# First batch's keys and queries loaded as 1152-byte pieces into w2's room, unpacked by copies and put in order at the multiplication; weight tiles taken in at other places

## The chip, the cores and the metric

The kernel runs on one core of a Trainium2 chip. The metric is the time of one execution on the device, in microseconds (us). Three executions of the kernel before gave 483.38, 480.39 and 482.63 us, median 482.63. A fourth was profiled: 480.19 us, of which 478.5 lie between its first and last instruction (the span). All times inside the kernel below are from that execution, counted from the start of the span.

## The reference

An attention-like recurrence over 4 batches, 8 heads, 768 steps and head dimension 48, followed by a mixer on 384 = 8 x 48 channels. Inputs are fp32 for q, k, v and f_logit as the profile's shapes show; the mixer's weights arrive as 64-bit floats and are turned into fp32 on the chip.

```python
f = 1.0 / (1.0 + np.exp(-f_logit))
for t in range(S):
    state = f[:, :, t, :, None] * state + np.einsum('bhd,bhe->bhde', k[:, :, t], v[:, :, t])
    y[:, :, t] = np.einsum('bhd,bhde->bhe', q[:, :, t], state)
x = y.transpose(0, 2, 1, 3).reshape(B, S, H * D)
h = x.transpose(0, 2, 1) @ U @ V
u = x + h.transpose(0, 2, 1)
out = u + np.maximum(u @ w_ch1, 0.0) @ w_ch2
```

## The kernel before, in words

**Units.** The attention works on pairs of heads: 4 pairs (HP) in each of 4 batches make 16 units, n = 0 to 15. A unit's 768 steps are cut into 12 chunks of 64. Within a chunk the recurrence is a masked product of scaled queries and keys (scores, L873; mask, L886); across chunks a scan carries the state (L943). The scale factors X and Y come from the gates f. Units 0 to 3 are the first batch and start the kernel; while units 4 and later are worked on, TensorE (PE) runs the mixer of the batch before.

**Loading.** The function load issues DMAs from SyncE (SP). For units 0 to 3 it brings f, k and q of one head as a tile of 128 partitions x 6 blocks x 48 values: step 128 c + p goes to partition p, block c (L592). One DMA per head and tensor, in pieces of 48 x 4 = 192 bytes, into two alternating slots, `late` and `other`, whose rows have 64 places per head. v is loaded by three DMAs per unit into v_nat (L592, L585). SP's order in this part is written out by hand (manual_schedule); later it is the framework's own. [...]

**A first-batch unit.** prepare(n) gives the front: logs (VectorE clips f, L731; ScalarE takes exp and ln, L733 and L734), log_sums (PE sums within chunks, L740), keep_logs (ScalarE makes X, L753, and Y, L754, and the chunk factors, L755 and L758), keys and queries. The last two are the function operand: PE transposes six blocks of 128 x 128 into PSUM (on_tensor, L710), and VectorE multiplies them by X or Y on the way out (L722). In PSUM, step 128 c + p stands at column p of block c, so the reading order is the order of time. attend(n) gives the rear: kept (PE transposes the keys back, L900; ScalarE copies, L904), spread (L910), scores and mask, states (PE, L921, with v; ScalarE copies the PSUM result, L928), scan (VectorE, L943), read (PE, L960; a small copy L967 that marks it done) and inner (PE, L978; ScalarE writes x, L984). The order of these pieces on PE, VectorE and ScalarE is written by hand in the loop `for n in range(HP)`. Units from 4 on take the gates by a sigmoid (L764 or L772) and two scans (L777 with the small L782 behind it, and L795); from unit 6 on VectorE transposes (L687) instead of PE, and L725 multiplies.

**Weights.** U, two parts of V, twelve tiles of w1 and twelve of w2 make 27 loads. Each has a start (the DMA, L82, into a buffer of 64-bit words) and an end: ScalarE twice (L91, L92), VectorE three times (L98, L99, L100) and GpSimd once (L101), which writes the fp32 tile. The first six w1 tiles land in buffers named zw, of which four come free after a small ScalarE copy (L1086, in held); the others share four buffers, w_raw. ahead_by(n, loads) makes calls that first start the load n places further on and then end their own. The main part's loop over `start + m.firsts[1:]` has 18 pieces; after each it calls the next load (two after the first), and what is left is called after the loop.

**Mixer of batch 0.** low_rank_of, added_up_of and mix_of (L218, L227, L243) add the low-rank part, turn_of and turn (L279, L255; ScalarE L281, L256) transpose, ch1_of and ch1 (L293, L267) make the first product, with ReLU on ScalarE (L310), and ch2 (L327) the second, whose sum VectorE adds to x (helper add, L197) and SP stores (L315). The ch1 products hold one of two PSUM buffers until L310 has read them. w1 is needed from 46 us, w2 from 102 us on.

Of the kernel before, what the change touches and what calls it, by code (L numbers as in the profile page):

```python
# [10 lines left out]
F32 = mybir.dt.float32  # L11
# [4 lines left out]
ALU = mybir.AluOpType  # L16
# [95 lines left out]
def ahead_by(n, loads):  # L112


    def call(i):
        if i + n < len(loads):
            loads[i + n][0]()
        loads[i][1]()

    return [lambda i=i: call(i) for i in range(len(loads))]  # L120
# [396 lines left out]
def factored_path(ctx, tc, q, k, v, f_logit, moe_U, moe_V, moe_w_ch1, moe_w_ch2, out, ok):  # L517
# [4 lines left out]
    nc = tc.nc  # L522
    B, H, S, D = q.shape
    P = nc.NUM_PARTITIONS
# [3 lines left out]
    NBL = S // P  # L528
    HP = H // 2
    DM = H * D  # L530
    R = moe_U.shape[1]
    FF = moe_w_ch1.shape[1]
    NDC = DM // P
# [37 lines left out]
    src = {"f": f_logit, "q": q, "k": k, "v": v}  # L571
    v_tiles = {}

    def load(n, *names):

        b, hp = divmod(n, HP)
        for nm in names:
            if nm == "v":
                v_tiles[n] = three.tile([P, NBL, 2, D], F32, name="v_nat")
            for par in range(2):  # L580
                head = src[nm][b, 2 * hp + par]
                if nm == "v" and par:

                    for s in range(2):
                        nc.sync.dma_start(  # L585
                            out=v_tiles[n][(1 - s) * C : (2 - s) * C, :, par, :],
                            in_=head.rearrange("(c s p) d -> s p c d", s=2, p=C)[s],
                        )
                    continue
                if nm == "v" or n < TURNED:  # L590
                    dst = v_tiles[n] if nm == "v" else nat[n % 2][nm]
                    nc.sync.dma_start(out=dst[:, :, par, 0:D], in_=head.rearrange("(c p) d -> p c d", p=P))  # L592
                    continue
                head = head.rearrange("(c i) d -> i c d", i=NB)
                for part in range(2):
                    p0 = par * PAD + part * NB
                    n_ch = min(NB, D - part * NB)
                    nc.sync.dma_start(
                        out=raw[n % 2][nm][p0 : p0 + NB, :].rearrange("p (c d) -> p c d", d=NB)[:, :, 0:n_ch],
                        in_=head[:, :, part * NB : part * NB + n_ch],  # L600
                    )
# [49 lines left out]
    for i in range(2):  # L651
        nc.gpsimd.memset(wholes[i][:, 0:1], 0.0)

    w1 = const.tile([P, NDC, FF], F32, name="w1")
    w2 = const.tile([P, NFC, DM], F32, name="w2")
    U = const.tile([P, NBL, R], F32, name="U")
    V = const.tile([P, (NBL * R + P - 1) // P, P], F32, name="V")
    take_in = weight_loader(nc, two, nc.sync)
# [34 lines left out]
    def prepare(n):  # L693
# [24 lines left out]

        def operand(nm, of):
            t = T[nm] = kz[n % 2][:, C:] if nm == "k" else two.tile([P, S], F32, name="qT")  # L720
            if n < TURNED:
                nc.vector.tensor_tensor(halves(t), on_tensor(nm), halves(T[of]), ALU.mult)  # L722
            else:
                turned(t, r[nm])
                nc.vector.tensor_tensor(t, t, T[of], ALU.mult)  # L725

        def logs():
            m = 2 if n == 0 else 1
# [70 lines left out]
            follow("q")  # L799

        if n < HP:
            return [logs, keep_logs, keys, log_sums, queries]
        return [gates, keep, keys, read, queries]

    x_tiles = {}
# [188 lines left out]
    def front(n, *names):  # L994

        if n >= NU:
            return []
        if n not in ahead:
            ahead[n] = dict(zip(("gates", "keep", "keys", "read_back", "queries"), prepare(n)))
        return [ahead[n].pop(nm) for nm in names]  # L1000

    def rear(n, *names):
# [59 lines left out]
    with tc.manual_schedule(engines={nc.vector.engine, nc.scalar.engine}):  # L1062


        idle = ps_mm.tile([P, 512], F32, name="idle", tag="mm")

        def busy(n, cols=DM):
            for _ in range(n):
                nc.tensor.matmul(idle[:, 0:cols], lhsT=blank[:, 0:P], rhs=blank[:, 0:cols], start=True, stop=True)

        written = ExitStack()
        written.enter_context(tc.manual_schedule(engines={nc.sync.engine}))
        busy(3)
        for piece in front(0, "gates", "read_back", "keep"):
            piece()
        load(1, "k", "q")
        load(2, "f")
        load(1, "v")
        loads = ahead_by(early + FIRST + 1, weights)
        halves, join = [[w[i] for w in weights[:early]] for i in (2, 3)]  # L1080
        done, rest = slice(0, 2 * (HP - 1) * D), slice(2 * (HP - 1) * D, DM)

        def held():
            for i in range(2, FIRST, 2):
                t = zp.tile([P, NFC // 2, 2 * P], F32, name="zw").rearrange("p i t -> p (i t)")
                nc.scalar.copy(t[:, 0:1], x_tiles[0][:, 0, 0:1])  # L1086
                spare.extend([t.bitcast(U64)[:, 0:WP], t.bitcast(U64)[:, WP : 2 * WP]])
            for load_w in weights[early + 2 : early + FIRST]:
                load_w[0]()
            load(HP, "f", "k", "q", "v")  # L1090

        for n in range(HP):
            last = n + 1 == HP
            pieces = rear(n - 1, "scan") + front(n, "keys") + rear(n, "spread") + rear(n - 1, "read")
            pieces += front(n, "queries") + (join[:1] if last else []) + rear(n, "kept")
            if n == 0:
                pieces += [lambda: busy(1, 2 * P)] + front(1, "gates") + rear(0, "scores", "mask", "states")
            elif last:
                pieces += halves[1:2] + join[1:2] + rear(n - 1, "inner") + [held] + halves[2:]
                pieces += rear(n, "states", "scan") + join[2:] + rear(n, "scores", "mask")  # L1100
            else:
                pieces += front(n + 1, "gates") + rear(n - 1, "inner") + rear(n, "states")
            if n + 2 == HP:
                pieces += halves[:1]
            if not last:
                pieces += front(n + 1, "read_back")
                pieces += rear(n, "scan", "scores", "mask") if n else []
                pieces += front(n + 1, "keep")
            for piece in pieces:
                piece()  # L1110
            if n == 0:
                load(2, "k", "q")
                load(3, "f")
                load(2, "v")
            elif n == 1:
                weights[0][0]()
                load(3, "k", "q")
                for load_w in weights[1:early]:
                    load_w[0]()
                load(3, "v")  # L1120
                for load_w in weights[early : early + 2]:
                    load_w[0]()
        m = mixer(0)
        low_rank_of, added_up_of, mix_of, turn_of, ch1_of = m.some
        for load_w in weights[early + FIRST : early + FIRST + 4]:
            load_w[0]()
        load(HP + 1, "f", "k", "q", "v")
        written.close()
        loads[early]()
        low_rank_of(done)  # L1130
        for piece in rear(n, "read"):
            piece()
        loads[early + 1]()
        added_up_of(done)
        for piece in rear(n, "inner"):
            piece()
        mix_of(done, range(0, NBL - 2, 2))
        low_rank_of(rest)
        mix_of(done, range(NBL - 2, NBL, 2))
        added_up_of(rest)  # L1140
        turn_of(0, range(2))
        mix_of(rest)
        ch1_of(0, 0, (0, 0), (0, 1))
        turn_of(0, range(2, NDC))
        ch1_of(0, 0, (1, 0), (1, 1))
        m.before[4][1]()
        ch1_of(0, 0, (0, 2), (1, 2))
        loads = loads[early + 2 :]
        loads.pop(0)()
        for t in fz:  # L1150
            nc.vector.memset(t[:, 0:S].rearrange("p (c t) -> p c t", t=C)[:, :, 0], 0.0)
            nc.vector.memset(t[:, S : S + 1], 0.0)

        start = m.before[5:]

        EARLY = 3
        second = chain(front(HP, "gates", "keep", "keys", "read_back", "queries"), steps(HP, 2 * HP + 1))
        for i, (_, piece) in enumerate(start + m.firsts[1:]):
            piece()
            for f in loads[: 2 if i == 0 else 1]:  # L1160
                loads.remove(f)
                f()
            if i >= EARLY:
                next(second)()
        for f in loads:
            f()
        n = len(m.seconds) // (NBL // 2)
        todo, after = m.seconds[:-n], m.seconds[-n:]

        attention(second, 12 + 10 * HP - (len(start) + len(m.firsts) - 1 - EARLY), todo)  # L1170
        m = start_mixer(1, after)
        for f in to_sum:
            f()
# [380 lines left out]
```

## Time and profile before

| | value |
|---|---|
| three executions, median (lowest to highest) | 482.63 us (480.39 to 483.38) |
| profiled execution, its span | 480.19 us, 478.5 us |
| mean granted TensorE clock | 0.994 of full |
| busy share of the span: PE, VectorE, ScalarE, GpSimd | 96%, 72%, 37%, 8% |
| chain that ended last: PE, VectorE, DMA, SP's queue, ScalarE | 79%, 9%, 3%, 3%, 2% |
| DMA moved, mean rate | 34.35 MB, 72 GB/s |
| packets, of these under 512 bytes | 158680, 149206 |

PE is TensorE's matmul queue and PEld its weight loads, DVE is VectorE, ACT is ScalarE, POOL is GpSimd, SPq is SP's queue of DMAs. A busy PE is not PE at its peak, and a share of busy time is a mean over stages with different limits: the first batch's attention (0 to about 46 us), ch1 of the first mixer (to 102), ch2 of it (to about 172), and the rest. A DMA share above 1 in a window means that packets queued in it are counted with their waiting. An fp32 matmul appears as two PE records. An instruction's bracket gives its engine's idle time before it and what ended that.

### The profile page before, as it was taken

Reading aid. Unit: us, or ns where it says so; the run is one execution under the profiler, and the core shown is the slowest. Engines: PE = TensorE matmul, PEld = TensorE weight load, DVE = VectorE, ACT = ScalarE, POOL = GpSimd, SP = SyncE. Lnnn points to the kernel's source line nnn. Section 1 sums busy time; section 2 is a strip of 40 time slices with the busy share of each in tenths; the row PEclk is TensorE's granted clock in tenths of the full one; section 3 lists DMA queues with packets and bytes.
Section 4 is the critical chain, followed back from the end, with each engine's and each line's share of the span. In section 5 each row is a group of like instructions: output and inputs, shape, how many; then the busy total and the mean of one; then the engine's idle time right before and its main releaser. Section 6 shows DMA issues by size and latency. Waiting matters only on the chain.

```text
span 478.5 us, 12782 instructions
## 1 busy us (share of the span) xinstructions
PE 461.5 (96%) x5547; PEld 399.2 (83%) x5547; DVE 346.4 (72%) x571; ACT 179.1 (37%) x327; POOL 36.1 (8%) x48
## 2 busy tenths in 40 slices
PE   7999999998999899999999999999999999999995
PEld 5876888875665478798899888899979999999995
DVE  4558688789999575667766547997796886858642
ACT  5775776664444123433341423542311311212200
POOL 2002245442000000000000000000000000000000
PEclk9999999998999999999999999999999999999998
DMA  9999987576777422253426200100000000000001
GB/s 144 161 167 225 217 174 188 133 155 92 119 118 117 84 41 26 26 77 77 67 39 100 38 33 3 27 4 21 16 1 1 34 1 18 18 0 34 1 34 39
DMA packets 158680, 34.35 MB, mean 72 GB/s; under 512 B 149206, under 2 KB 157078, under 8 KB 158614
## 3 DMA queue, kind: packets, MB, share of 16 engines
q1 hardware_dynamic: 158614, 33.44, 37.8%
q8 instruction: 45, 0.74, 0.7%
q14 instruction: 21, 0.17, 0.1%
HBM read 28.70 MB, written 4.72 MB: 70 GB/s over the span
## 4 chain that ended last, share of the span: by engine, by line
PE 79%; DVE 9%; DMA 3%; SPq 3%; ACT 2%; issue 2%; POOL 0%; DVEq 0%; ACTq 0%; POOLq 0%
PE pw L356 26%; PE pz L267 22%; PE pp L454 12%; PE po L327 4%; PE sc L873 2%; DMA v_nat<-in_v_dram 2%; PE y L960 2%; PE y L978 2%; PE put L255 2%; PE ds L921 1%; PE pt L900 1%; PE pt L710 1%; SPq L592 1%; DVE late L795 1%; PE pu L207 1%
## 5 line engine op out<-in xcount | busy, mean ns | idle before, releaser
L267 PE MATMUL pz<-uT,w 128*128 128x256 f32 x492 | 111.3, 382 | 1.1 <-ACT z_all L310 1.1
L267 PEld LDWEIGHTS pz<-uT,w 128*128 128x128 f32 x492 | 91.7, 190 | 13.9 <-ACT z_all L310 1.5
L356 PE MATMUL pw<-w,z_all 128*128 128x192 f32 x216 | 37.7, 329 | 0.0
L356 PE MATMUL pw<-zw,w_raw 128*128 128x192 f32 x216 | 37.3, 327 | 0.0
L356 PEld LDWEIGHTS pw<-zw,w_raw 128*128 128x128 f32 x216 | 35.2, 190 | 0.7 <-DVE w_raw L197 0.6
L310 ACT ACTIVATE z_all<-pz 128x512 f32<-128x512 f32 x33 | 19.7, 598 | 42.6 <-PE pz L267 42.5
L356 PEld LDWEIGHTS pw<-w,z_all 128*128 128x128 f32 x216 | 35.0, 190 | 0.7
L101 POOL TENSOR_TENSOR w<-w_y,w_r 128x384 int32<-128x384 int32 x24 | 31.5, 1313 | 40.5 <-DVE w_y L100 27.1
L948 ACT COPY st<-added 128x576 f32<-128x576 f32 x12 | 14.7, 1225 | 39.7 <-DVE added L943 39.7
L454 PE MATMUL pp<-v_nat,late 128*128 128x128 f32 x224 | 28.8, 275 | 0.0
L327 PE MATMUL po<-w,zw 128*128 128x384 f32 x72 | 25.3, 496 | 2.0 <-POOL w L101 2.0
L454 PEld LDWEIGHTS pp<-v_nat,late 128*128 128x128 f32 x224 | 27.0, 192 | 0.0
L327 PE MATMUL po<-w,z_all 128*128 128x384 f32 x72 | 25.0, 495 | 1.6 <-DVE o L197 1.6
L447 ACT ACTIVATE other<-other 128x512 f32<-128x512 f32 x18 | 11.3, 631 | 39.9 <-DVE other L197 39.9
L886 DVE TENSOR_TENSOR A<-sc,causal 128x768 f32<-128x768 f32 x16 | 15.2, 951 | 12.2 <-PE sc L873 12.1
L777 DVE TENSOR_TENSOR_SCAN late<-fz,late 128x768 f32<-128x768 f32 x12 | 21.1, 1755 | 4.0 <-ACT fz L772 3.6
L327 PEld LDWEIGHTS po<-w,zw 128*128 128x128 f32 x72 | 13.1, 190 | 11.6 <-POOL w L101 2.6
L327 PEld LDWEIGHTS po<-w,z_all 128*128 128x128 f32 x72 | 13.4, 192 | 10.6 <-DVE o L197 2.2
L795 DVE TENSOR_TENSOR_SCAN late<-fz,other 128x768 f32<-128x768 f32 x12 | 21.0, 1747 | 0.2
L98 DVE TENSOR_SCALAR w_y<-w_y 128x384 f32<-128x384 f32 (+3 forms) x27 | 12.3, 456 | 11.1 <-ACT w_y L91 11.1
L447 ACT ACTIVATE z_all<-z_all 128x512 f32<-128x512 f32 x12 | 7.6, 630 | 32.8 <-DVE z_all L197 32.8
L928 ACT COPY added<-ds 48x576 f32<-48x576 f32 (+1 forms) x28 | 17.8, 636 | 4.9 <-PE ds L921 4.8
(220 smaller groups left out, 851.3 us busy)
## 6 DMA issues: line engine op xcount, KB each, us to landing
w_raw<-in_moe_w_ch_dram SPq DMA_DIRECT2D x18, 384.0 KB, 3.8
out_dram<-o SPq DMA_DIRECT2D x24, 192.0 KB, 1.9
v_nat<-in_v_dram SPq DMA_DIRECT2D x16, 144.0 KB, 3.9
v_nat<-in_v_dram SPq DMA_DIRECT2D x32, 72.0 KB, 3.8
zw<-in_moe_w_ch_dram SPq DMA_DIRECT2D x6, 384.0 KB, 5.4
late<-in_f_logit_dram SPq DMA_DIRECT2D x10, 96.0 KB, 3.0
late<-in_k_dram SPq DMA_DIRECT2D x10, 96.0 KB, 2.8
late<-in_q_dram SPq DMA_DIRECT2D x10, 96.0 KB, 2.6
```

The source lines that it names most:

```text
L101: nc.gpsimd.tensor_tensor(dst.bitcast(I32), shaped(y.bitcast(I32)), shaped(r), ALU.add)
L267: nc.tensor.matmul(pm[:, i * 2 * P : (i + 1) * 2 * P], lhsT=w1[:, m, o : o + P], rhs=uT[a][:, m, :], start=(m == 0), stop=(m == NDC - 1))
L310: nc.scalar.activation(z[a, c][:, k : k + 2, :].rearrange("p i t -> p (i t)"), pm, AF.Relu)
L327: nc.tensor.matmul(pm, lhsT=z[a, i // NI][:, i % NI, s * P : (s + 1) * P], rhs=w2[:, i, :], start=(i == 0), stop=(i == NFC - 1))
L356: nc.tensor.matmul(pm[:, n * HM : (n + 1) * HM], lhsT=lhs[:, i, :], rhs=rhs[:, i, :], start=(i == 0), stop=(i == NI - 1))
L447: nc.scalar.activation(dst, dst, AF.Relu, scale=float(SIGNS[n]))
L454: nc.tensor.matmul(pm[:, i, r * P : (r + 1) * P], lhsT=room["w"](wn)[:, r * P : (r + 1) * P], rhs=x_node(a, xn), start=((xn, wn) == of[0]) ...
L777: nc.vector.tensor_tensor_scan(backwards(X, S - 1, S), backwards(f, S, S), backwards(ends, S - 1, S), 0.0, ALU.mult, ALU.add,)
L795: nc.vector.tensor_tensor_scan(Y, f[:, 0:S], starts, 0.0, ALU.mult, ALU.add)
L886: nc.vector.tensor_tensor(T["A"], sc[:, :, 0 : NBL * C].rearrange("p h (c i) -> p h c i", i=C), causal.unsqueeze(1).unsqueeze(1).broadcast ...
L928: nc.scalar.copy(added[r, 1:].rearrange("p (e c s) -> p e c s", c=NBL, s=2), ds[r, :, 0 : NBL * D].rearrange("p s (c e) -> p e c s", e=D),)
L948: nc.scalar.copy(st, states.rearrange(by_e, c=NCH))
```

## The change

It has two parts.

**k and q of units 0 to 3.** load issues one DMA for both heads of a tensor instead of two. Step 6 p + c now goes to partition p, place c, so each partition receives six consecutive steps of a head, 288 values or 1152 bytes in one piece. The target is a region of w2's tile, which is not used before its weights come (eight regions of 576 values fill its 4608 values per partition), so w1 and w2 are allocated earlier in the program. A new piece, unpack (L747 in the changed kernel), has VectorE copy each tensor into the old slot's shape, twice per unit: for unit 0 behind its clipping, for unit 1 behind unit 0's mask, for units 2 and 3 behind their clipping. After PE's transposes, step 6 p + c stands at column p of block c. So the multiplication (L737 in the changed kernel, in the place of L722) reads PSUM in the order column, then half, then block, and both its other operand and its result stay in the order of time. f and v are loaded as before. PE's instructions and their order are unchanged.

**Weight tiles.** loads are started 11 places ahead instead of 10 (early is 3 and FIRST is 6, so 9 + 2 for 9 + 1). The DMA of w1's tile 10 (counted from 0) is issued between k and q of unit 5 instead of after unit 5. The third w1 tile's end moves ahead of two transposing steps. The loop calls two loads after its first and its third piece, so that one load instead of two is left after the loop. ScalarE's and VectorE's orders change in just these places.

```diff
+    w1 = const.tile([P, NDC, FF], F32, name="w1")
+    w2 = const.tile([P, NFC, DM], F32, name="w2")
+
+    def packed(n, nm):
+
+        i = 2 * n + (nm == "q")
+        return w2.rearrange("p c d -> p (c d)")[:, i * 2 * NBL * D : (i + 1) * 2 * NBL * D]
+
     def load(n, *names):
...
                 head = src[nm][b, 2 * hp + par]
+                if nm in "kq" and n < HP:
+                    if par == 0:
+                        nc.sync.dma_start(
+                            out=packed(n, nm).rearrange("p (h t) -> p h t", h=2),
+                            in_=src[nm][b, 2 * hp : 2 * hp + 2].rearrange("h (p c) d -> p h (c d)", p=P),
+                        )
+                    continue
...
         def operand(nm, of):
             t = T[nm] = kz[n % 2][:, C:] if nm == "k" else two.tile([P, S], F32, name="qT")
-            if n < TURNED:
+            if n < HP:
+                pt = on_tensor(nm).rearrange("p a c t -> p a (c t)").rearrange("p a (c t) -> p t a c", c=NBL // 2)
+                by_time = "p (t a c) -> p t a c"
+                nc.vector.tensor_tensor(t.rearrange(by_time, a=2, c=NBL // 2), pt,
+                                        T[of].rearrange(by_time, a=2, c=NBL // 2), ALU.mult)
+            elif n < TURNED:
                 nc.vector.tensor_tensor(halves(t), on_tensor(nm), halves(T[of]), ALU.mult)
...
+        def unpack():
+            for nm in "kq":
+                nc.vector.tensor_copy(
+                    nat[n % 2][nm][:, :, :, 0:D], packed(n, nm).rearrange("p (h c d) -> p c h d", h=2, c=NBL),
+                )
...
-        for piece in front(0, "gates", "read_back", "keep"):
+        for piece in front(0, "gates", "unpack", "read_back", "keep"):
...
-        loads = ahead_by(early + FIRST + 1, weights)
+        loads = ahead_by(early + FIRST + 2, weights)
...
-                pieces += [lambda: busy(1, 2 * P)] + front(1, "gates") + rear(0, "scores", "mask", "states")
+                pieces += [lambda: busy(1, 2 * P)] + front(1, "gates") + rear(0, "scores", "mask") + front(1, "unpack")
+                pieces += rear(0, "states")
...
-                pieces += front(n + 1, "gates") + rear(n - 1, "inner") + rear(n, "states")
+                pieces += front(n + 1, "gates", "unpack") + rear(n - 1, "inner") + rear(n, "states")
...
-        load(HP + 1, "f", "k", "q", "v")
+        load(HP + 1, "f", "k")
+        weights[early + FIRST + 4][0]()
+        load(HP + 1, "q", "v")
...
         turn_of(0, range(2, NDC))
+        loads[early + 2]()
         ch1_of(0, 0, (1, 0), (1, 1))
         m.before[4][1]()
         ch1_of(0, 0, (0, 2), (1, 2))
-        loads = loads[early + 2 :]
-        loads.pop(0)()
+        loads = loads[early + 3 :]
...
-            for f in loads[: 2 if i == 0 else 1]:
+            for f in loads[: 2 if i in (0, 2) else 1]:
```

More of the change, by code (lines that the diff above doesn't have):

```diff
@@ L652, in factored_path @@
         nc.gpsimd.memset(wholes[i][:, 0:1], 0.0)
-    w1 = const.tile([P, NDC, FF], F32, name="w1")
-    w2 = const.tile([P, NFC, DM], F32, name="w2")
     U = const.tile([P, NBL, R], F32, name="U")
@@ L801, in prepare @@
         if n < HP:
-            return [logs, keep_logs, keys, log_sums, queries]
+            return [logs, keep_logs, keys, log_sums, queries, unpack]
         return [gates, keep, keys, read, queries]
@@ L998, in front @@
         if n not in ahead:
-            ahead[n] = dict(zip(("gates", "keep", "keys", "read_back", "queries"), prepare(n)))
+            ahead[n] = dict(zip(("gates", "keep", "keys", "read_back", "queries", "unpack"), prepare(n)))
         return [ahead[n].pop(nm) for nm in names]
```

## The prediction

> **What bounds the kernel now.** First the windows view, to find the stages. Columns: stretch, length, busy us of PE, PE's weight loads, VectorE, ScalarE and GpSimd with instruction counts, TensorE clock, DMA share, GB/s.
>
> ```profile
> 10.00:15.00 5.00, 4.62 (x125) 4.04 (x121) 2.81 (x4) 3.30 (x6) 0.00 (x0) 1.00 1.46 163
> 20.00:25.00 5.00, 4.99 (x139) 4.38 (x130) 3.18 (x3) 3.87 (x9) 0.00 (x0) 1.00 0.88 151
> 105.00:110.00 5.00, 5.00 (x104) 3.31 (x103) 3.39 (x7) 3.99 (x9) 1.84 (x2) 1.00 1.00 135
> 110.00:115.00 5.00, 3.04 (x61) 1.78 (x63) 4.90 (x8) 0.00 (x0) 2.31 (x1) 0.90 0.65 95
> 115.00:120.00 5.00, 5.00 (x73) 3.70 (x66) 4.96 (x6) 3.15 (x4) 0.00 (x0) 0.76 0.48 62
> ```
>
> The DMA engines are full in the first 20 us, yet PE is hardly short of work there. From 50 to 110 us PE is at 5.00 of 5. The hole is at 110 to 115, and the clock falls with it.
>
> Then the timeline at that hole, engine by engine (start, us, engine, line; the bracket is idle time before and its releaser):
>
> ```profile
> 107.42 3.49 PE L327 MATMUL po<-w,zw 128*128 128x384 f32 x10
> 112.87 0.91 PE L327 MATMUL po<-w,zw 128*128 128x384 f32 x2 [1.96 <-POOL w L101]
> 113.71 1.33 PE L978 MATMUL y<-v_nat,A 64*64 64x48 f32 x48
> ...
> 108.55 1.00 POOL L101 TENSOR_TENSOR w<-w_y,w_r 128x384 int32<-128x384 int32 x1 [2.71 <-ACT seen L967]
> 110.50 2.31 POOL L101 TENSOR_TENSOR w<-w_y,w_r 128x384 int32<-128x384 int32 x1 [0.95 <-DVE w_y L100]
> ...
> 107.06 0.36 DVE L98 TENSOR_SCALAR w_y<-w_y 128x384 f32<-128x384 f32 x1 [1.47 <-ACT w_y L91]
> 108.33 0.35 DVE L98 TENSOR_SCALAR w_y<-w_y 128x384 f32<-128x384 f32 x1
> 110.28 1.75 DVE L777 TENSOR_TENSOR_SCAN late<-fz,late 128x768 f32<-128x768 f32 x1
> ```
>
> PE's last ch2 product waits 1.96 us for the last w2 tile. Two tiles are joined after the loop (VectorE 107.06 and 108.33), and behind them VectorE starts its next unit only at 110.28.
>
> Last, the timeline of the first batch:
>
> ```profile
> 8.50 0.85 PE L710 MATMUL pt<-ident,late 128*128 128x128 f32 x6 [0.15 <-DMA late<-in_q_dram]
> 12.30 0.90 PE L921 MATMUL ds<-v_nat,kb 64*64 64x48 f32 x42 [0.38 <-DMA v_nat<-in_v_dram]
> 19.55 0.90 PE L921 MATMUL ds<-v_nat,kb 64*64 64x48 f32 x42 [0.39 <-DMA v_nat<-in_v_dram]
> 28.61 1.61 PE L740 MATMUL pt<-later,other 128*128 128x130 f32 x12 [0.47 <-ACT other L734]
> 21.39 1.36 DVE L943 TENSOR_TENSOR_SCAN st<-added,whole 128x576 f32<-128x576 f32 x1 [2.54 <-ACT added L928]
> 29.66 1.36 DVE L943 TENSOR_TENSOR_SCAN st<-added,whole 128x576 f32<-128x576 f32 x1 [2.54 <-ACT added L928]
> ```
>
> DMA costs PE directly only 0.15 + 0.38 + 0.39, and some 0.6 more at 35.8, where the 24 products of L921 take 1.58 instead of 1.0 us until unit 3's v has landed. VectorE has holes of 2.54 us ahead of the scans.
>
> [...] L722 shows 952[...]. [...] (ScalarE's L948 reads 48 bytes apart: 1225 ns for 576, against 672 for L910) [...] ScalarE's L928 reads PSUM with steps of 2 KB and takes 635. [...] In 5 to 10 us, with pieces of 192 B only, the trace has 169 GB/s; in 36 to 44, mostly the 1 KB pieces of w1, 270. [...] L101 shows 1.00 us alone and 2.31 beside the scan L777.
>
> **The change part by part.** The sum is made against the profiled execution, 480.19 us with a span of 478.5; the median of the three runs is 482.63, 2.4 above it.
>
> *Loads.* Sixteen k and q DMAs of 192-byte pieces become eight of 1152-byte pieces. SP issues one in about 0.55 us, so it gains 8 x 0.55 = 4.4 us by unit 3. The 2.36 MB need 14 us at 169 GB/s and, at the 270 of the 1 KB pieces, about 9 (estimate). Unit 0's q should land near 7 us instead of 8.5, and each v moves ahead by more than the 0.4 to 0.6 us that PE waits for it. Nothing else is queued behind a new wait: the new DMAs go to room of their own.
>
> *Unpack.* Two copies of 576 elements per unit: 2 x 0.45 = 0.9 us of VectorE, 3.6 in all [...]. They stand after the max L731, in unit 1 after the mask L886. Units 2 and 3 fall into the 2.54 us holes. Unit 0 falls between 5.7 and 8.63, where VectorE waits for L753. Unit 1: the mask ends at 12.9, the copies at 13.8, the scan wants to start at 13.5 to 13.9. So nothing, or 0.3 at the upper price. Without these holes it would be 3.6. [...]
>
> *Multiplications L722.* Eight of them now read PSUM 512 bytes apart[...]; their SBUF sides stay contiguous. Nearest row: L928, no penalty on ScalarE. [...] I take 0.
>
> *What the first batch gains.* Without the v wait at 12.30 PE reaches L740 at 12.75 instead of 13.12. At 19.55 another 0.39 goes, but L740 of unit 2 then needs ScalarE's L734 of unit 2, so in sum 0.4, not 0.8. From 20.4 to 28.1 PE is full, and the 0.4 is kept. At the end v of unit 3 is in time; next late is ScalarE, which must first do the parts of V (L91, L92 until 37.14, where L928 began at 37.48): 0.3 more. Sum 0.75 us at 46.
>
> *Weight tiles.* The third w1 tile moves from ScalarE's slot at 50.97 to one at 48.46, where its data is in and PE's L255 is still running. Its join leaves the hole of 4.20 us before VectorE's L98 at 51.55. One tile per 1.95 us is the pace from 53 to 63 (VectorE and GpSimd in turn), so this saves nearly one pace, and the second tile now put in at the third piece spends it again. VectorE's scan at 65.76 stays where it was, and PE's 50 to 110 stays full: L310 has a slack of about 1 us at its PSUM buffers. From there every tile is in its predecessor's slot; its DMA has moved one place ahead in SP's queue too, keeping some 10 us of lead (for example 70.0 to 80.9). The tile put between k and q of unit 5 waits for its buffer until about 59.3, and may hold q back 1 us; that q is used at 92.
>
> At the end only one tile is left after the loop, in the slot of 107.06. GpSimd starts at 108.55 and, beside the scan, takes 2.31: 110.86, while PE wants it at 110.9. So the 1.96 goes, and with it the slow stretch: L978 1.33 for 0.91, L873 1.54 for 0.89, L900 0.90 for 0.59, L327 4.27 for 4.14, together 1.5. PE gains 0.75 + 1.96 + 1.5 = 4.2 us.
>
> But VectorE gains less: L777 starts at 108.33 instead of 110.28, 1.95, plus 0.75 = 2.7. From 121 to 163 it works 11.2 of every 12.1 us and idles only 0.9 for L772. PE waits for it at 155.28 (0.38) and at 163.12 (1.64, L197), so PE's surplus is given back there. After 163 PE is full and everything moves by 2.7.
>
> Sum: 478.5 - 2.7 = 475.8 of span; 480.2 - 2.7 = 477.5 for the execution; against the median 482.6 - 2.7 = 479.9.
>
> **Rivals.** *PE's gain survives* (0.2): if VectorE's chain behind 121 us loosens too, for instance because the clash with GpSimd at 112 (L782, 0.78 instead of 0.17) goes, 3.5 to 4.2 us stay: about 478.7. Against it: the 0.9 us idles are the only slack.
>
> *Hidden anyway* (0.15): the last tile is late again, because a tile's DMA comes late behind the pieces of f, k, q in SP's queue, or ScalarE falls behind L310 near 63 us. Then only the front's 0.75 or less stays: 482.
>
> *Strided PSUM read, slower* (0.13): each L722 costs 0.8 more. In unit 0 both lie on the path to L734 of unit 1 (1.5); then the q one delays the max, L733, L734 and PE's L740 by 0.8 per unit (1.6), and the last delays U's join and the scores (about 1.3): 4.4. 482.6 - 2.7 + 4.4 = 484.3. The change turns to a loss when the penalty exceeds about 0.5 us an instruction. Against it: L928.
>
> **How the numbers follow.** The likeliest, 0.5, is 2.7 us: 479.9, own range 478.5 to 481.5. The other 0.02 is for a load that isn't in time. The range reaches from the surviving PE gain, with its spread, to the strided read: 477.0 to 484.8. A measurement of this kernel can tell about 1% (4.8 us) from no change. Faster by over 1% needs more than the whole of PE's gain: 0.10. Slower by over 1% needs the strided read together with a stall: 0.07. Within: 0.83.
>
> **What would show it.** L737 at 0.95 us and L747 at 0.45 (or 1.75 and 0.75); no wait of PE on v; GpSimd's last L101 starting near 107.8 and L327 unbroken; a clock of 1.00 at 110 to 120; VectorE's scan near 107.6; PE still waiting for L197 near 160. I am wrong if the multiplications lengthen, or if PE gets a hole between 50 and 110.

## The result, and the profile after

| | before | after |
|---|---|---|
| median, nine executions each | 480.39 us (480.21 to 487.57) | 478.01 us (477.45 to 480.27) |
| profiled execution, its span | 480.19 us, 478.5 us | 477.89 us, 476.2 us |
| mean granted TensorE clock | 0.994 | 0.998 |
| packets, of these under 512 bytes | 158680, 149206 | 148312, 136790 |
| chain that ended last: PE, VectorE | 79%, 9% | 75%, 13% |

The ratio is 0.9943, with a 95% interval of 0.992 to 0.9966: faster by 0.6%, clear of no change by the interval, though less than the 1% that the prediction took for what one measurement can tell. The 487.57 of before is an execution in a slower state and does not enter the ratio. The span fell by 2.3 us; 2.7 was predicted. The predicted 479.9 lies 1.9 above the median mainly because it was set on a median of three, 482.63, which nine executions put at 480.39.

Windows of the kernel after, with the columns of those shown of before:

```profile
10.00:15.00 5.00, 4.80 (x130) 4.04 (x125) 3.81 (x6) 3.91 (x7) 0.00 (x0) 1.00 1.21 217
110.00:115.00 5.00, 4.93 (x117) 3.41 (x117) 4.93 (x8) 1.21 (x1) 0.19 (x1) 1.00 0.77 103
115.00:120.00 5.00, 4.44 (x102) 2.95 (x101) 4.45 (x6) 2.40 (x5) 0.00 (x0) 1.00 0.75 94
```

In the first batch the DMA engines deliver 217 GB/s where they gave 163. At 110 to 115 us PE is busy 4.93 of 5 instead of 3.04, and the clock stays at 1.00. But a new hole of 0.56 has come at 115 to 120 (PE 4.44 of 5).

The timeline at the old hole, PE, GpSimd and VectorE:

```profile
106.69 4.47 PE L327 MATMUL po<-w,zw 128*128 128x384 f32 x12
111.09 0.92 PE L1002 MATMUL y<-v_nat,A 64*64 64x48 f32 x48
118.70 0.76 PE L945 MATMUL ds<-v_nat,kb 64*48 64x48 f32 x48 [0.56 <-issue]
...
107.88 2.31 POOL L101 TENSOR_TENSOR w<-w_y,w_r 128x384 int32<-128x384 int32 x1 [2.72 <-DVE w_y L100]
...
106.39 0.36 DVE L98 TENSOR_SCALAR w_y<-w_y 128x384 f32<-128x384 f32 x1 [1.47 <-ACT w_y L91]
107.66 1.75 DVE L801 TENSOR_TENSOR_SCAN late<-fz,late 128x768 f32<-128x768 f32 x1
```

(The kernel after has other line numbers: L801, L1002, L945, L984, L764, L952, L967, L910 and L758 there are L777, L978, L921, L960, L740, L928, L943, L886 and L734 of before.) One tile is joined after the loop, GpSimd has it at 110.19, and the twelve records (six products) run without a gap. They take 4.47 us where twelve take 4.14 further on, since the last two weight loads still come behind that tile, at 110.25 with 0.68 us of idle time on PEld that it ends: it is just in time. VectorE's scan comes at 107.66 for 110.28, 2.62 us earlier; PE's L1002 at 111.09 for 113.71, also 2.62.

The first batch in the kernel after:

```profile
12.54 1.61 PE L764 MATMUL pt<-later,other 128*128 128x130 f32 x12
19.95 1.61 PE L764 MATMUL pt<-later,late 128*128 128x130 f32 x12 [0.59 <-ACT late L758]
28.19 1.61 PE L764 MATMUL pt<-later,other 128*128 128x130 f32 x12 [0.58 <-ACT other L758]
38.78 1.24 PE L984 MATMUL y<-st,qT 48*64 48x48 f32 x44 [1.14 <-DVE w_y L98]
6.89 0.46 DVE L747 COPY late<-w 128x576 f32<-128x576 f32 x1 [0.53 <-DMA w<-in_q_dram]
8.66 0.96 DVE L737 TENSOR_TENSOR kz<-pt,late 128x768 f32<-128x768 f32 x1 [0.73 <-ACT late L777]
21.00 1.36 DVE L967 TENSOR_TENSOR_SCAN st<-added,whole 128x576 f32<-128x576 f32 x1 [1.62 <-ACT added L952]
29.23 1.36 DVE L967 TENSOR_TENSOR_SCAN st<-added,whole 128x576 f32<-128x576 f32 x1 [1.80 <-ACT added L952]
```

No wait of PE on v or q is left. A copy takes 0.46, a multiplication that reads PSUM out of order 0.96, and the holes ahead of the scans shrink from 2.54 to 1.62 and 1.80. What is late now at 20 and 28 is ScalarE, and at 38.78 the scan behind ScalarE's L952 (the bracket names an L98 that stands between them on VectorE).

### The profile page after: what moved, and what is told of

The parts are those of the page before. It is cut to its first block, busy times and chain, and to the rows that moved or that the text cites. A ratio compares the mean times of both kernels' runs of the same rounds, so it can differ in the third digit from the quotient of the medians.

```text
span 476.2 us, 12778 instructions
## 1 busy us (share of the span) xinstructions
PE 459.8 (97%) x5547; PEld 397.5 (83%) x5547; DVE 349.0 (73%) x579; ACT 179.1 (38%) x327; POOL 36.1 (8%) x48
## 2 busy tenths in 40 slices
DMA packets 148312, 34.35 MB, mean 72 GB/s; under 512 B 136790, under 2 KB 146710, under 8 KB 148246
## 4 chain that ended last, share of the span: by engine, by line
PE 75%; DVE 13%; DMA 3%; issue 3%; ACT 3%; SPq 2%; POOL 0%; DVEq 0%
PE pw L356 26%; PE pz L267 22%; PE pp L454 12%; PE sc L897 2%; DVE late L819 2%; PE po L327 2%; PE y L984 2%; PE put L255 2%; PE y L1002 1%; DVE added L967 1%; PE pt L924 1%; DVE late L801 1%; PE pu L207 1%; PE pt L764 1%; SPq L600 1%
## 5 line engine op out<-in xcount | busy, mean ns | idle before, releaser
L267 PE MATMUL pz<-uT,w 128*128 128x256 f32 x492 | 111.4, 382 | 1.1 <-ACT z_all L310 1.1
L267 PEld LDWEIGHTS pz<-uT,w 128*128 128x128 f32 x492 | 91.7, 190 | 14.0 <-ACT z_all L310 1.5
L101 POOL TENSOR_TENSOR w<-w_y,w_r 128x384 int32<-128x384 int32 x24 | 31.5, 1311 | 38.8 <-DVE w_y L100 23.5
L327 PE MATMUL po<-w,z_all 128*128 128x384 f32 x72 | 24.9, 493 | 1.6 <-DVE o L197 1.6
L327 PE MATMUL po<-w,zw 128*128 128x384 f32 x72 | 25.3, 496 | 0.1
L910 DVE TENSOR_TENSOR A<-sc,causal 128x768 f32<-128x768 f32 x16 | 15.2, 951 | 12.2 <-PE sc L897 11.9
L801 DVE TENSOR_TENSOR_SCAN late<-fz,late 128x768 f32<-128x768 f32 x12 | 21.1, 1755 | 4.0 <-ACT fz L796 3.6
L327 PEld LDWEIGHTS po<-w,z_all 128*128 128x128 f32 x72 | 13.3, 190 | 10.5 <-DVE o L197 2.3
L327 PEld LDWEIGHTS po<-w,zw 128*128 128x128 f32 x72 | 13.1, 190 | 9.8 <-issue 1.2
L984 PEld LDWEIGHTS y<-st,qT 48*64 48x64 f32 x704 | 13.5, 137 | 7.1 <-issue 4.5
L952 ACT COPY added<-ds 48x576 f32<-48x576 f32 (+1 forms) x28 | 17.8, 636 | 3.9 <-PE ds L945 3.7
```

Of the source, the lines that this page charges most:

```text
L101: nc.gpsimd.tensor_tensor(dst.bitcast(I32), shaped(y.bitcast(I32)), shaped(r), ALU.add)
L267: nc.tensor.matmul(pm[:, i * 2 * P : (i + 1) * 2 * P], lhsT=w1[:, m, o : o + P], rhs=uT[a][:, m, :], start=(m == 0), stop=(m == NDC - 1))
L327: nc.tensor.matmul(pm, lhsT=z[a, i // NI][:, i % NI, s * P : (s + 1) * P], rhs=w2[:, i, :], start=(i == 0), stop=(i == NFC - 1))
L801: nc.vector.tensor_tensor_scan(backwards(X, S - 1, S), backwards(f, S, S), backwards(ends, S - 1, S), 0.0, ALU.mult, ALU.add,)
L910: nc.vector.tensor_tensor(T["A"], sc[:, :, 0 : NBL * C].rearrange("p h (c i) -> p h c i", i=C), causal.unsqueeze(1).unsqueeze(1).broadcast ...
L952: nc.scalar.copy(added[r, 1:].rearrange("p (e c s) -> p e c s", c=NBL, s=2), ds[r, :, 0 : NBL * D].rearrange("p s (c e) -> p e c s", e=D),)
```

## The experiments

Each has its own comparison with the kernel before on its chip; the median of before there was 481.7 in the first four, 481.21 in the others. Single executions of one kernel differ by some us, so marks inside the trace are used beside the medians. The first is the time at which PE reaches L293, the mixer's first ch1 product that follows the first batch (46.70 in before, 45.84 in after). The second is the stretch from there to the start of ch2's L327 that waits for L197: 163.12 - 46.70 = 116.42 in before, 160.52 - 45.84 = 114.68 in after. The first shows the loads' half, the second the tiles' half; a fall of TensorE's clock lengthens the one it comes in (the second by 1.7 us when the kernel before was profiled once more, below).

**The loads alone.** The kernel after with these lines set back:

```diff
-        loads = ahead_by(early + FIRST + 2, weights)
+        loads = ahead_by(early + FIRST + 1, weights)
...
-        load(HP + 1, "f", "k")
-        weights[early + FIRST + 4][0]()
-        load(HP + 1, "q", "v")
+        load(HP + 1, "f", "k", "q", "v")
...
-        loads[early + 2]()
...
-        loads = loads[early + 3 :]
+        loads = loads[early + 2 :]
+        loads.pop(0)()
...
-            for f in loads[: 2 if i in (0, 2) else 1]:
+            for f in loads[: 2 if i == 0 else 1]:
```

> The changed kernel with the weight tiles' part taken back: k and q in 1152-byte pieces, unpacked, but every weight tile where it was before. My theory (two separate gains that add): PE is 0.8 to 0.9 us earlier at 46 us, as in the changed kernel, but two tiles are again left after the loop, so GpSimd's last L101 starts near 109.7 and PE waits about 2 us for it, with the clock falling again. Span near 478.5 - 0.8 = 477.7, ratio to before 0.998. Rival (the loads make the tiles' part possible or bring most of the gain): 476.5 or less, and no wait for the last tile.

Measured: 480.02 us, ratio 0.995 (0.993 to 0.997), span 477.9. L293 at 46.12, the stretch 162.53 - 46.12 = 116.41, just that of before. The timeline shows the old wait, PE and GpSimd:

```profile
112.28 0.91 PE L327 MATMUL po<-w,zw 128*128 128x384 f32 x2 [1.96 <-POOL w L101]
107.97 0.99 POOL L101 TENSOR_TENSOR w<-w_y,w_r 128x384 int32<-128x384 int32 x1 [2.71 <-ACT seen L991]
109.92 2.31 POOL L101 TENSOR_TENSOR w<-w_y,w_r 128x384 int32<-128x384 int32 x1 [0.96 <-DVE w_y L100]
```

So the loads give 0.6 us here at L293 (0.86 in the kernel after), and nothing behind it. The difference between the two lies ahead of unit 1: VectorE gets f of unit 0 at 4.93 here and at 4.55 there, and from unit 1's L764 to L293 both take 33.30 us (12.82 to 46.12, 12.54 to 45.84). That the clock would fall again was expected and did not happen, as the window behind the wait shows:

```profile
115.00:120.00 5.00, 5.00 (x71) 3.06 (x70) 4.97 (x6) 3.14 (x4) 0.00 (x0) 1.00 0.51 66
```

The medians differ by 1.7 us and the ratio is worth 2.4, more than these marks explain. Most of the rest goes with the clock. Among the executions whose mean granted clock was 0.998 or more (10 of the loads alone, 11 of before), the medians are 480.02 and 480.86, 0.84 apart. Why the loads alone had fewer executions with a lower clock stays open.

**The tiles alone,** twice: before, with the lines above set the other way.

> The kernel before with only the weight tiles moved, k and q loaded as before. My theory: PE's waits for v and q in the first batch stay (0.15, 0.38, 0.39 and some 0.6), PE is at its old place at 46 us; at the end no wait for the last tile, VectorE's scan behind it starts near 108.4 instead of 110.28, and everything after 163 us moves by 1.8 to 1.95. Span near 476.6, ratio 0.996. Rival (the moved tiles need the room that the shorter loads make in SP's queue): a hole of PE between 50 and 110 us or a late last tile, and a span of 478 or more.

> The weight tiles' half alone once more, to see whether the 1.5 us by which the first batch ended later than in the profile of the kernel before belongs to that half or to the execution. If it belongs to the execution: PE at L293 between 46.5 and 48.3, other than 48.19, and from there to the last ch2 product's L327 near 162 again 114.7 us; ratio to the kernel before 0.996. If it belongs to the half: again 48.2, with v of unit 3 late.

Measured: 480.24 us, ratio 0.9962 (0.9943 to 0.9981), span 478.3; again 480.12 us, ratio 0.9975 (0.9957 to 0.9993), span 477.0. The first span missed what was expected by 1.7. Its PE timeline in the first batch shows why:

```profile
36.98 0.28 PE L921 MATMUL ds<-v_nat,kb 64*64 64x48 f32 x2 [1.14 <-ACT zw L1086]
37.42 1.04 PE L921 MATMUL ds<-v_nat,kb 64*64 64x48 f32 x45 [0.16 <-DMA v_nat<-in_v_dram]
```

v of unit 3 comes about 1.1 us later than in before's profile (the last product that needs it starts at 38.30 for 37.22): SP issues its DMAs from 31.82 on, in the second execution of the same kernel from 29.61. Behind PE's wait the clock fell, and L218 took 2.13 us where it takes 1.16:

```profile
38.00:40.00 2.00, 2.00 (x89) 1.60 (x81) 0.77 (x1) 1.44 (x3) 0.13 (x1) 0.69 0.98 303
40.00:42.00 2.00, 2.00 (x28) 0.79 (x24) 1.93 (x5) 0.44 (x2) 0.45 (x1) 0.50 0.97 303
```

So L293 is at 48.19; in the second execution it is at 46.8, with the clock at 1.00. The lateness belongs to the execution, part of it to the arrival of v and part to the clock. The stretch is 162.89 - 48.19 = 114.70 and 161.50 - 46.8 = 114.7, as in the kernel after: the tiles give 1.7 us. With the loads' 0.6 to 0.86 that makes the whole 2.3 to 2.6: two gains that add, as expected.

**The kernel before, profiled once more.**

> The kernel before, profiled once more, to see how much the arrival of its 192-byte pieces differs between executions. If arrivals differ by execution, PE reaches L293 at another time than 46.70, up to 48.2, with waits on v of 0.2 to 1.2 us at other places than before; from L293 to L327 near 163 it is 116.4 again, and the last w2 tile is waited for by 2.0 us. If not, all is at 46.70 within 0.1.

Measured: 481.58 us, ratio 0.9999 (0.9976 to 1.0023), span 480.3. L293 is at 46.8, so arrivals differed little this time, though the waits stand elsewhere (0.18 on q at 16.60, 0.60 on v at 19.77, 0.36 on v at 35.87; none near 12.3, where the state products take 1.24 us for 0.87 instead). From L293 to L327 it is 164.87 - 46.76 = 118.1 and not the 116.4 that was expected. That is nearly all of the 1.8 by which the span lies above the first profile's, and it comes from the clock:

```profile
46.00:48.00 2.00, 2.00 (x16) 1.60 (x15) 1.14 (x3) 0.32 (x1) 0.00 (x0) 0.76 0.64 126
48.00:50.00 2.00, 2.00 (x7) 1.61 (x6) 0.00 (x0) 0.37 (x1) 0.00 (x0) 0.50 1.23 199
...
115.00:120.00 5.00, 5.00 (x113) 3.92 (x112) 4.96 (x5) 1.84 (x3) 0.00 (x0) 0.66 0.54 69
```

It falls to 0.50 behind the first batch as well, where it had stayed at 1.00. The median of L293's records is 600 ns instead of 379, and from L293 to the first L267 PE takes 1.7 us longer (5.94 for 4.23).

**The copies twice.**

```diff
-            for nm in "kq":
+            for nm in "kqkq":
```

> The changed kernel with each unpacking copy done twice, the result the same: 3.6 us more of VectorE. My theory (the copies are covered where VectorE waits for ScalarE, except little in unit 1): units 2 and 3 hide the second pair too, in what is left of their holes (1.62 and 1.80 us); unit 0 loses 0.1 to 0.3; in unit 1, where the first pair just fits, the second delays the scan by 0.8 to 0.9. Together 0.9 to 1.2 us: span near 477.2. If the copies were on the path: 479.8 (all 3.6). If there were room everywhere: 476.2.

Measured: 478.76 us, ratio 0.9945 (0.9924 to 0.9967), span 476.9: 0.7 more than after, L293 0.75 later. Timeline, unit 1:

```profile
15.72 1.24 PE L984 MATMUL y<-st,qT 48*64 48x48 f32 x44 [0.70 <-DVE st L967]
12.84 1.56 DVE L747 COPY other<-w 128x576 f32<-128x576 f32 x4
14.31 1.35 DVE L967 TENSOR_TENSOR_SCAN st<-added,whole 128x576 f32<-128x576 f32 x1
```

Doubling 3.6 us of copies costs 0.7 us (0.9 to 1.2 was expected), all of it in unit 1, where the scan starts at once behind the copies. In the kernel after, PE waits 0.19 there (14.99); the other three units cover even the doubled copies.

**One DMA for each head, the pieces of 1152 bytes kept.**

```diff
-                    if par == 0:
-                        nc.sync.dma_start(
-                            out=packed(n, nm).rearrange("p (h t) -> p h t", h=2),
-                            in_=src[nm][b, 2 * hp : 2 * hp + 2].rearrange("h (p c) d -> p h (c d)", p=P),
-                        )
+                    nc.sync.dma_start(
+                        out=packed(n, nm)[:, par * NBL * D : (par + 1) * NBL * D],
+                        in_=head.rearrange("(p c) d -> p (c d)", p=P),
+                    )
```

> The changed kernel with one DMA for each head's k and q instead of one for both, with the same 1152-byte pieces: sixteen DMAs again. My theory (the size of the pieces brings v in time, not the number of DMAs): PE waits for no v and no q in the first batch, and the span is that of the changed kernel, 476.2, within 0.3. Rival (the eight saved issues at 0.5 us each on SP bring it): waits for v at units 0 or 1 come back, 0.4 us or more, span 476.6 to 477.

Measured: 478.49 us, ratio 0.9943 (0.9921 to 0.9965), span 476.7; L293 at 46.43; no wait of PE on v or q. So the waits are gone without the eight issues saved (SP takes 0.47 to 0.61 us for one of them in the kernel after): it is the size of the pieces that brings v in time. But the span missed the 0.3 us given for it and lies in the rival's range. The 0.5 us between it and after's arises ahead of L293 (0.6 there): 0.2 before 12.7 us, and 0.4 in unit 3, where VectorE's multiplication of q starts at 34.20 (33.60 in after) and the trace names only "issue" for its wait. Whether that belongs to the eight issues or to the execution stays open.

**VectorE's gates ahead of the mask.** In the kernel after, from 111 to 160 us, the chain of waits runs mainly through VectorE. This experiment changes VectorE's order there and leaves PE's work and its order as they are. (In this kernel and the next L943, L982, L965 and L908 are L945, L984, L967 and L910 of the kernel after.)

```diff
             T["sc"] = sc
-            if b:
-                mask()
...
-            yield from front(n + 1, "gates", "keep", "keys")
+            gates, masked = front(n + 1, "gates"), rear(n - 1, "mask")
+            yield lambda: [f() for f in gates + masked]
+            yield from front(n + 1, "keep", "keys")
```

> The kernel after, with one order changed on VectorE: in each of the units' pieces from batch 1 on, the transposition of the next unit's gates (L700) stands ahead of the mask (L910) of the unit before, instead of behind it. It tests the step that PE's surplus from the weight tiles is given back to VectorE between 111 and 163 us. In that stretch VectorE idles only 0.9 us per unit, for the sigmoid L796 that follows L700. Theory (VectorE's order sets the pace): the sigmoid comes earlier, the 0.9 disappears from four units, so VectorE arrives some 3 us earlier at L197 near 160.5, PE's 1.64 us wait there goes, and PE loses some 0.6 to 0.9 at the state products behind the later mask: span 474.6, 1.6 below the kernel after. Rival (something else takes the surplus): span 476.2, with the 1.64 wait moved to another place. Other side: the later mask holds up PE in each unit, and the span is 477 or more.

Measured: 476.66 us (476.03 to 480.36), ratio 0.9906 (0.9875 to 0.9937). The profiled execution took 480.36, with a clock of 0.50 from 42 to 50 us, so its span, 478.6, does not say what the order is worth. From L293's last start to the end it takes 478.6 - 53.1 = 425.5, in the kernel after 476.2 - 49.2 = 427.0: 1.5 less, of 1.6 expected.

**Gates ahead, and L952 ahead of V's second part.** The second edit:

```diff
-                pieces += halves[1:2] + join[1:2] + rear(n - 1, "inner") + [held] + halves[2:]
-                pieces += rear(n, "states", "scan") + join[2:] + rear(n, "scores", "mask")
+                pieces += halves[1:2] + join[1:2] + rear(n - 1, "inner") + [held] + rear(n, "states")
+                pieces += halves[2:] + rear(n, "scan") + join[2:] + rear(n, "scores", "mask")
```

> As the one with the gates ahead of the mask, and one order more on ScalarE: in unit 3 the copy of the state products L952 stands ahead of the second part of V (L91, L92 near 36.2 us). In the kernel after PE waits 1.14 us at 38.78 for the scan that follows L952. Theory (ScalarE's parts of V are what is late at the end of the first batch): L952 and the scan come 0.6 us earlier, PE's wait falls from 1.14 to about 0.5, and all behind 46 us moves by 0.6: PE at L293 at 45.2 instead of 45.84, span 0.6 below the one with the gates alone (474.0). Rival: V itself is then late for L243 near 41.6, and the gain is 0.

Measured: 475.69 us, ratio 0.9879 (0.9834 to 0.9924), span 473.9 (474.0 expected), L293 at 45.0. The timeline of PE and VectorE:

```profile
37.76 1.24 PE L982 MATMUL y<-st,qT 48*64 48x48 f32 x44 [0.44 <-DVE st L965]
...
118.72 0.76 PE L943 MATMUL ds<-v_nat,kb 64*48 64x48 f32 x48 [1.43 <-ACT fz L796]
...
117.70 0.92 DVE L908 TENSOR_TENSOR A<-sc,causal 128x768 f32<-128x768 f32 x1
118.67 1.76 DVE L801 TENSOR_TENSOR_SCAN late<-fz,late 128x768 f32<-128x768 f32 x1
...
156.94 0.81 PE L190 MATMUL ph<-h,blocks 128*128 128x384 f32 x2
157.75 4.14 PE L327 MATMUL po<-w,z_all 128*128 128x384 f32 x12
```

The wait at 38.78 has shrunk from 1.14 to 0.44. VectorE's scan at 118.67 has no idle time before it; in the kernel after it waits 0.90 there (120.38). That idle time is gone in two units, 0.17 in a third, and stays 0.90 in the fourth (153.14); four had been expected. At 118.72 PE waits 1.43 instead of 0.56: the state products start 0.1 us after the moved mask ends on VectorE (117.70 + 0.92 = 118.62; the bracket names a sigmoid on another engine). Behind that PE is without a wait up to 163, and the 1.64 us for L197 is gone. An order on VectorE gave what PE could not keep by itself: in the kernel after it is VectorE that sets the pace of this stage. With the order changed PE does, from 118.72 on.

**After and the version with both orders on one chip.**

> The kernel after, on the same chip as the version with two orders changed, to compare the two directly. Expected: span 475.7 to 477 according to the clock of the execution, PE at L293 near 45.8, ratio to the kernel before 0.994, and the waits of 1.14 us at 38.8 and of 1.64 us for L197 near 160.5 there again. If instead it comes within 0.5 us of the version with both orders, that version's gain belonged to its chip and not to the orders.

> The kernel after with the gates' transposition ahead of the mask and with L952 ahead of the second part of V, once more, beside the kernel after. Expected: span 473.9, PE at L293 near 45.0 to 45.2, ratio to the kernel before 0.989, and 2.2 us (1.5 for the gates, 0.6 to 0.8 for the state copy) below the median of the kernel after on this chip. If the gain were the chip's, the two medians would be within 0.5 us.

Measured: after 478.06 us (477.41 to 481.7), ratio 0.9939 (0.9923 to 0.9955), span 476.0, L293 at 45.7, the waits of 1.14 and 1.64 there again. Both orders: 476.48 us (476.03 to 478.63), ratio 0.9909 (0.9879 to 0.994), span 474.3, L293 at 45.5. The gap is 1.7 us of span and 1.6 of median, where 2.2 was expected, so the gain is not the chip's. Stretches inside the traces give each order's part. From L293's last start to the end it is 425.4 to 425.5 in all three traces with the gates ahead and 427.0 in both of after: 1.5. From L218 to L293 it is 8.87 in both traces with L952 ahead (36.16 to 45.03, 36.65 to 45.52) and 9.36 in both of after (36.48 to 45.84, 36.30 to 45.66): 0.5, since of the 0.70 by which the wait for the scan shrinks a new wait of 0.26 at L227 takes a part. The rest is the way up to L218, which differs between executions: from L764 of unit 3 it took 36.65 - 27.95 = 8.70 us, with an idle of 0.23 at 30.64 whose cause the trace does not name, where it had been 36.16 - 27.87 = 8.29. That the first execution of both orders met the expected 474.0 is in part luck: 0.3 of its lead over after lay ahead of L218. This version is the best one measured, ahead of both kernels.

## Why the prediction was right, step by step

*Loads.* Right. q of unit 0 is at VectorE's copy at 6.89 (near 7 was predicted), no v is waited for, and the piece size carries it. The delivered rate is 217 to 224 GB/s; the estimate from the w1 pieces was 270, but f and v still come in pieces of 192 bytes. In 5 to 10 us the rate rose from 169 to 224 with only k and q enlarged. "Full in the first 20 us" was too wide: the DMA share of the kernel before is 0.67 in the first 5 us, then 1.48, 1.46 and 1.04.

*Unpack.* Right: 0.46 for a copy of 576 elements, as L731's 0.45 for 576 in the kernel before; the upper price, 0.75, is what VectorE's sums of 576 at L197 take there (746 ns). Units 0, 2 and 3 are covered. Unit 1 is the tight one, as predicted; PE's wait there is 0.19, inside the 0 to 0.3 given. That the copies are covered by idle time, and not free, shows when they are doubled.

*The strided read of PSUM.* Right: L737 takes 0.95 to 0.96, as the contiguous L722 did (0.952). VectorE's read at steps of 512 bytes pays nothing here, and neither had ScalarE's L928 at steps of 2 KB: 643 ns for 128 x 576 in the kernel before, where L984's reading of 128 x 576 in PSUM without such steps takes 636. The rival of a slower read, which needed 0.5 us an instruction, is out. The 0.8 us that it put on each was the author's estimate; VectorE's sums at L197 in the kernel before (746 ns for 576 elements, 948 for 768, so 1.05 ns an element) would make 0.81 for a second pass over 768.

*The first batch's gain.* 0.86 for 0.75 in the profile of after; 0.58 with the loads alone and 1.0 in the second profile of after, so the close hit is partly chance. Both halves of the step show: no wait at 12.3, and a better end. The end was ScalarE's order, as said, and moving L952 takes the wait from 1.14 to 0.44.

*Weight tiles.* Right in place and size: one tile after the loop, GpSimd at 107.88 (107.8 predicted) for 2.31, PE without a gap, VectorE's scan at 107.66 (107.6). The tile put between k and q of unit 5 left SP at 58.81 and q followed at 59.27 instead of 58.34, 0.9 us later (1 was predicted); PE has no wait from 50 to 110. One point was off: the scan at 65.76 was to stay where it was, and came at 65.35.

*The slow stretch.* Here the sum took a chance for a certainty. The 1.5 us by which the clock stretched PE's work after the wait were counted as the wait's price. With the loads alone the same wait of 1.96 leaves the clock at 1.00; in the two profiles of before it fell to 0.76 and 0.66. It cost the sum nothing, because that part was to be given back anyway: the loads alone, at full clock, take 116.41 us from L293 to L327, and the first profile of before, with the clock at 0.76, took 116.42.

*The surplus given back.* Right in cause, wrong in place. PE in the kernel before, then PE in the kernel after, then VectorE in the kernel after:

```profile
121.31 0.84 PE L960 MATMUL y<-st,qT 48*64 48x48 f32 x42
155.28 1.48 PE L182 MATMUL ph<-x,U 128*32 128x384 f32 x12 [0.38 <-ACT x L984]
163.12 3.17 PE L327 MATMUL po<-w,z_all 128*128 128x384 f32 x9 [1.64 <-DVE o L197]
...
117.24 0.90 PE L984 MATMUL y<-st,qT 48*64 48x48 f32 x44
130.83 0.76 PE L945 MATMUL ds<-v_nat,kb 64*48 64x48 f32 x48 [0.33 <-issue]
152.68 1.49 PE L182 MATMUL ph<-x,U 128*32 128x384 f32 x12 [0.53 <-ACT x L1008]
160.52 4.14 PE L327 MATMUL po<-w,z_all 128*128 128x384 f32 x12 [1.64 <-DVE o L197]
...
117.65 0.95 DVE L910 TENSOR_TENSOR A<-sc,causal 128x768 f32<-128x768 f32 x1
120.38 1.76 DVE L801 TENSOR_TENSOR_SCAN late<-fz,late 128x768 f32<-128x768 f32 x1 [0.90 <-ACT fz L796]
```

PE was 4.07 us ahead at 117.24 (L984; 4.2 predicted) and 2.60 at 152.68. The prediction had the surplus lost at 155.28 and 163.12. But the waits there are nearly as long in both kernels, 0.38 and 0.53, 1.64 and 1.64. Of the 1.47 lost, 0.77 and 0.54 go at the state products at 118.70 and 130.83, with new waits of 0.56 and 0.33 ahead of L945, and 0.16 at 152.68. The trace names only "issue" for the new waits. L945 starts 0.1 us after the mask L910 ends in the kernel after (117.65 + 0.95 = 118.60), and in the version with both orders PE comes 0.85 earlier, the mask ends at the same time (118.62), and the products start 0.1 behind it again. So they wait for the mask. The program fits that: the scores, the transposed keys, y and the state products take turns in a pool of three PSUM buffers (ps_big), so that the state products come into the one that the mask has to read. No run with a fourth buffer tests it.

*The end.* The shift of 2.6 at 160.52 reaches the last VectorE instruction; some 0.3 is lost between it and the end of the span, in the final store.

The rival that PE's gain survives (3.5 to 4.2) is out: 2.6 at 160 us. So is the one that everything is hidden. The median alone would not have told them apart: 478.01 lies below the 478.5 to 481.5 given for the likeliest case and nearest to the 478.7 of the first rival, because the median of before came down by 2.2 us. The span tells: 475.8 was predicted, 476.2 measured.

## What to carry to other kernels

When a wait on the bounding engine goes, follow the gain to the next place where another engine sets the pace: here 4.1 us on PE became 2.6 within 35 us, because VectorE had gained only that. Then look at that engine's order: moving one transposition ahead of one mask brought 1.5 us, more than half as much as the whole change. And before a difference of 1 or 2 us between two profiles is believed, compare stretches between marks inside each trace, since the start and the clock differ from one execution to the next.

## What the runs showed of the hardware

TensorE's clock falls in some executions and not in others behind the same idle time. Windows around the end of the first batch, in the version with the gates ahead:

```profile
38.00:40.00 2.00, 0.94 (x43) 0.97 (x44) 1.93 (x5) 0.76 (x3) 0.26 (x1) 1.00 0.82 224
40.00:42.00 2.00, 2.00 (x62) 1.49 (x53) 1.92 (x5) 1.37 (x4) 0.33 (x2) 0.82 0.96 312
42.00:44.00 2.00, 2.00 (x28) 1.02 (x20) 1.94 (x3) 0.64 (x1) 1.04 (x2) 0.50 1.13 283
44.00:50.00 6.00, 6.00 (x31) 4.13 (x28) 2.57 (x5) 1.06 (x3) 0.81 (x1) 0.50 0.96 154
```

The longest wait of PE there is the 1.14 us that the kernel after has too, with a clock of 1.00; the loads alone have PE busy for the same 0.94 of 2.00 us in that first window and keep 1.00. The fall stretched L293's twelve records from 3.4 to 5.1 us between first and last start. Of the five falls that the windows show, four came behind a wait of 1.14 to 1.97 us; the one at 46 us in the second profile of the kernel before had no wait of PE over 0.45 in the 20 us ahead of it. Waits of 1.96 (the loads alone) and 1.14 (the kernel after) passed without a fall. No run here shows what decides.

GpSimd's L101 takes 1.00 us alone. Started 0.2 us behind a scan of VectorE it takes 2.31 to 2.33 where the scan takes 1.75, five times each in the traces of the kernels before and after, and 1.92 where the scan takes 1.35 (88.79 and 88.56 us in the kernel after). In both cases it ends 0.8 us after the scan does: with the scan 0.40 shorter, L101 was 0.39 shorter. VectorE's small copy behind the longer scan (L806) takes 0.78 there and ends with L101, where it takes 0.17 without it.
